# A pre-norm attention and feed-forward block on one core: seven half products for two row blocks, and q,k,v in 512 and 448 columns

## The chip, the cores and the metric

The kernel runs on one core of one Trainium2 chip. The metric is the device time of one execution in microseconds (us). The profile of one execution gives the times of its instructions; the engines are PE (matrix products), DVE and ACT (vector and scalar work), POOL, and SP, which here only issues DMAs.

## The reference

For `x` of 2048 rows and 640 columns: h = x + attention(layernorm(x)), result = h + ffn(layernorm(h)).

```python
def _A_ref(x, wqkv, wo):            # H = 32 heads of Dh = 20; W, dil = 8, 2
    qkv = (x @ wqkv) ...            # q, k, v of each head
    idx = pos[:, None] - (arange(W) * dil)[None, :]     # a row attends to itself and 7 rows before it, every second
    logits = einsum("bhsd,bhswd->bhsw", q, kg) * scale  # idx < 0 is masked
    o = einsum("bhsw,bhswd->bhsd", softmax(logits), vg)
    return o.reshape(B, S, D) @ wo

def _B_ref(x, w_gate, w_up, w_down):                    # 640 -> 1728 -> 640
    return (silu(x @ w_gate) * (x @ w_up)) @ w_down
```

Every matrix product is done in three passes: each operand is held as a rounded high part and the remaining low part, and high x high, high x low and low x high are added up in one bank. A contraction over 640 takes five chunks of 128, so a product tile takes 15 matmuls.

## The kernel before

The rows are four blocks (0 to 3) of 512; a block is four row tiles `j` of 128. `first` and `last` run q,k,v for all blocks (`qkv(b, g)`, L575): `g` is one of four column groups, each with 160 columns of q, 160 of k and 160 of v, 480 in all, four row tiles, 15 matmuls each. ACT scales and stores the product to `stage` (L580); k, v and q go to DRAM (`ksc`, `vsc`, `qsc`). Attention runs on DVE in 16 groups (block and column group): `att_qk` multiplies and reduces (L623, L628, two of each), `att_exp` and ACT's exponential (L641), `att_av` multiplies and adds (L654, L663) and turns the result (L670), which goes to DRAM as `osc` (40 KB pieces).

`wo(b)` reads `osc` back, splits it (L736 ACT, L737 DVE) and multiplies by the output weights (L747: 8 products of 15 matmuls, 320 columns); the sum with `x` is `h`; layernorm follows. Blocks 2 and 3 are turned into columns by `turn`: a 32x32 transpose on DVE (L491), four DMAs to DRAM (`xsc`, L493) and one back. `turned_columns` splits the columns into `shb` (L486, L487); blocks 0 and 1 are transposed on PE (L444, L447, L448).

`ffn(b)` goes over 14 tiles of 128 of the 1728 inner columns (the last has 64). For each, `load_ffn` reads the weights (960 KB), ACT makes the high parts (L785, L786), DVE the low ones (L802; in block 0 they are stored to `lsc`, and blocks 1 and 2 read them from there), `proj` makes gate and up (L810, 2 x 15 matmuls of 512 columns, banks 5 and 6), ACT takes silu (L844), DVE multiplies (L845), ACT and DVE split the result (L846, L848), and `down` adds 15 matmuls of 512 columns into banks 0 to 4 (L826). `finish(b)` adds `h` (L875, L879) and writes out.

All operations are recorded by `P.add(engine, cost, function, reads, writes, prio)` and ordered by `P.order()`: a list schedule with the given costs, passes backward and forward, and small seeded moves (`MOVES`). Each engine works its own list in that order, and the reads and writes become semaphore waits. So `wo(b + 1)` and the attention of later blocks lie between the tiles of block `b`. `fa`, `ra`, `sha`, `shb`, `kv` and `pq` are large areas that stages share; `kv` and `pq` belong to attention.

## Time and profile before

| | |
|---|---|
| median of 3 runs | 859.25 us (859.12 to 859.33) |
| the profiled execution | 859.15 us, its span 857.1 us |
| mean granted TensorE clock | 0.999 |
| PE busy | 850.7 us, 4007 matmuls recorded |
| DVE busy | 643.5 us |
| ACT busy | 405.7 us |
| HBM | read 140.92 MB, written 43.65 MB |

A row of a group reads: line, engine, operation, output <- input, shape, count | busy us, mean ns of one | idle us before, and who ended it. A row of the waits reads: engine, line <- who was waited for: us in total, times, longest. A row of a stretch reads: start:end, length, and busy us (count) of PE, weight loads, DVE, ACT, POOL, then granted clock, DMA share and GB/s. A row of DMA issues ends with KB of each and the median us to landing.

### The profile page before, as it was taken

The page shows a single profiled execution, that of the slowest core. Times are in us where ns is not written, and L with a number is a line of the kernel's source. Part 1 is how long each engine was busy: PE and PEld are TensorE (multiplying, and loading weights), DVE is VectorE, ACT ScalarE, POOL GpSimd, SP SyncE. Part 2 cuts the span into 40 slices and gives each one's busy share as a digit, 9 for nine tenths or more (in the row PEclk, how much of TensorE's full clock was granted, in tenths as well). Part 3 has the DMA queues.
Part 4 walks back from the last instruction along what each step waited for, and adds up shares of the span by engine and source line. Part 5 has one row for each costly group of instructions (what it writes and reads, how often), then busy time and mean ns, then how long its engine had stood idle before and what let it go on. Part 6 is the DMA issues. An engine that isn't in the chain of part 4 may idle for free.

```text
span 857.1 us, 10563 instructions
## 1 busy us (share of the span) xinstructions
PE 850.7 (99%) x4007; PEld 723.4 (84%) x4007; DVE 643.5 (75%) x705; ACT 405.7 (47%) x658; POOL 2.5 (0%) x10
## 2 busy tenths in 40 slices
PE   9999999999999999999999999999999999999998
PEld 7888888889988888988888898888888888888886
DVE  6599999999988999989999987899722326334333
ACT  6875484233762434574434548443434725233321
POOL 0000000000000000000000000000000000000000
PEclk9999999999999999999999999999999999999999
DMA  7997688569697787667999995799882756322201
GB/s 248 277 311 232 183 245 223 138 192 269 182 301 252 219 282 239 185 211 273 324 278 303 266 297 155 257 286 282 250 300 75 211 196 207 129 92 93 93 31 61
DMA packets 80018, 185.27 MB, mean 216 GB/s; under 512 B 28880, under 2 KB 42448, under 8 KB 79200
## 3 DMA queue, kind: packets, MB, share of 16 engines
q1 hardware_dynamic: 79968, 184.60, 69.9%
q8 instruction: 31, 0.51, 0.3%
q14 instruction: 19, 0.16, 0.1%
HBM read 140.92 MB, written 43.65 MB: 215 GB/s over the span
## 4 chain that ended last, share of the span: by engine, by line
PE 98%; DMA 1%; SPq 0%; ACT 0%; DVE 0%; issue 0%
PE bank L810 43%; PE bank L575 24%; PE bank L826 22%; PE bank L747 8%; PE bank L444 1%; DMA fa<-in_wqkv_dram 1%; PE bank L868 0%; PE bank L530 0%; SPq L476 0%; DVE h L875 0%; ACT ra L549 0%; ACT shb L447 0%; SPq L546 0%
## 5 line engine op out<-in xcount | busy, mean ns | idle before, releaser
L810 PE MATMUL bank<-shb,ra 128*128 128x512 f32 x1620 | 386.7, 390 | 0.4 <-ACT shb L447 0.4
L810 PEld LDWEIGHTS bank<-shb,ra 128*128 128x128 f32 x1620 | 303.4, 188 | 62.9 <-ACT shb L447 0.8
L826 PE MATMUL bank<-ra,acts 128*128 128x512 f32 x656 | 167.1, 391 | 0.0
L826 PEld LDWEIGHTS bank<-ra,acts 128*128 128x128 f32 x656 | 122.5, 188 | 24.7
L845 DVE TENSOR_TENSOR fa<-bank,fa 128x512 f32<-128x512 f32 x52 | 35.8, 689 | 107.4 <-PE bank L810 92.0
L575 PE MATMUL bank<-ra,sha 128*128 128x480 f32 x480 | 107.0, 381 | 0.2 <-ACT ra L549 0.2
L575 PE MATMUL bank<-ra,shb 128*128 128x480 f32 x470 | 103.0, 379 | 0.0
L575 PEld LDWEIGHTS bank<-ra,sha 128*128 128x128 f32 x480 | 89.4, 188 | 13.7 <-ACT ra L549 0.5
L575 PEld LDWEIGHTS bank<-ra,shb 128*128 128x128 f32 x470 | 88.1, 188 | 13.1
L785 ACT CAST ra<-fa 128x1280 fp32r<-128x1280 f32 (+1 forms) x56 | 68.5, 1224 | 50.8 <-PE bank L810 39.4
L663 DVE TENSOR_TENSOR pq<-pq 128x1280 f32<-128x1280 f32 (+2 forms) x96 | 89.7, 934 | 2.4
L623 DVE TENSOR_TENSOR pq<-kv,pq 128x2560 f32<-128x2560 f32 x32 | 90.3, 2822 | 0.9 <-DMA kv<-ksc 0.4
L654 DVE TENSOR_TENSOR pq<-kv,pq 128x2560 f32<-128x2560 f32 x32 | 90.3, 2822 | 0.7
L628 DVE TENSOR_REDUCE pq<-pq 128x128 f32<-128x2560 f32 x32 | 90.0, 2813 | 0.4
L802 DVE TENSOR_TENSOR ra<-fa,ra 128x640 fp32r<-128x640 f32 (+1 forms) x82 | 65.6, 819 | 23.2 <-ACT ra L786 21.6
L844 ACT ACTIVATE fa<-bank 128x512 f32<-128x512 f32 x52 | 31.1, 598 | 94.1 <-PE bank L810 89.3
L747 PE MATMUL bank<-ra 128*128 128x320 f32 x480 | 75.0, 310 | 0.0
L747 PEld LDWEIGHTS bank<-ra 128*128 128x128 f32 x480 | 72.0, 188 | 2.9 <-ACT fa L750 1.3
L580 ACT ACTIVATE st<-bank,fa 128x480 f32<-128x480 f32 x64 | 41.5, 662 | 67.1 <-PE bank L575 63.7
L786 ACT CAST ra<-fa 128x640 fp32r<-128x640 f32 x56 | 40.5, 726 | 59.0 <-PE bank L826 58.9
L846 ACT CAST acts<-fa 128x512 fp32r<-128x512 f32 x52 | 32.3, 621 | 58.6 <-DVE fa L845 58.5
L826 PE MATMUL bank<-acts,ra 128*128 128x512 f32 x164 | 46.1, 390 | 0.0
(88 smaller groups left out, 493.0 us busy)
## 6 DMA issues: line engine op xcount, KB each, us to landing
fa<-in_ffn_dram SPq DMA_DIRECT2D x52, 960.0 KB, 6.4
ra<-lsc SPq DMA_DIRECT2D x26, 640.0 KB, 5.3
kv<-ksc SPq DMA_DIRECT2D x32, 440.0 KB, 6.4
kv<-vsc SPq DMA_DIRECT2D x32, 440.0 KB, 7.1
ra<-lsc SPq DMA_DIRECT2D x30, 320.0 KB, 4.4
lsc<-ra SPq DMA_DIRECT2D x13, 640.0 KB, 6.0
ksc<-st SPq DMA_DIRECT2D x32, 160.0 KB, 3.2
qsc<-st SPq DMA_DIRECT2D x16, 320.0 KB, 4.0
```

What stands on the lines that cost most here:

```text
L575: T.matmul(banks[bk][:, 0:480], l, r_(wq(g, w, c), 480), start=(p, c) == first_mm, stop=(p, c) == last_mm)
L580: P.add("ACT", act(480) + 0.06, lambda bk=bk, j=j: A.activation(stage_t()[:, so : so + 1920].rearrange("p (t j c) -> p t j c", t=3, j=NJ)[ ...
L623: P.add("DVE", dve(2560), lambda: V.tensor_tensor(pq(PROD, 2560).rearrange("p (j w c) -> p j w c", j=2, w=W), window(ko, 2 * jp), pq(qo + ...
L628: P.add("DVE", dve(2560), lambda: V.tensor_reduce(pq(lo + 128 * jp, 128), pq(PROD, 2560).rearrange("p (n d) -> p n d", d=DH), axis=AX.X, o ...
L654: V.tensor_tensor(pq(PROD, 2560).rearrange("p (j n d) -> p j n d", j=2, d=DH), bass.AP(tensor=v.tensor, offset=v.offset, ap=[list(v.ap[0]) ...
L663: V.tensor_add(dst(v), v[:, :, 0:m, :], v[:, :, m : 2 * m, :])
L747: T.matmul(banks[bk][:, 0:320], l, r_(m, 320), start=p == 0 and c == 0, stop=p == 2 and c == NC - 1)
L785: P.add("ACT", act(n), lambda: A.copy(r_(gu, n), f(raw, n)), r=[rf(raw, n)], w=[rr(gu, n)], prio=PR["fh"])
L786: P.add("ACT", act(640), lambda: A.copy(r_(dn[0], 640), f(raw + n, 640)), r=[rf(raw + n, 640)], w=[rr(dn[0], 640)], prio=PR["fh"])
L802: P.add(eng, c, lambda o=o: E.tensor_sub(ra[p0:, lo + o : lo + o + 640], fa[p0:, raw + o : raw + o + 640], ra[p0:, hi + o : hi + o + 640]. ...
L810: T.matmul(banks[bk], r_(gu + 1280 * w + wid * c + col, 128), x2(a, c), start=p == 0 and c == 0, stop=p == 2 and c == NC - 1)
L826: T.matmul(banks[k], l, m, start=first and p == 0, stop=last and p == len(passes) - 1)
```

## The change

q,k,v: groups 2 and 3 together, and in blocks 1 to 3 also groups 0 and 1, are multiplied as 512 and 448 columns instead of twice 480; 32 columns of the second group's q ride with the first. They are evicted and written by an instruction of their own.

Feed-forward of blocks 2 and 3: tiles 0 to 7 of block 2 run as before (`classic`). Tiles 8 to 12 are made for both blocks at once by `pair_tile`. It splits four of the five chunks of the contraction into two halves and makes gate and up of both blocks from seven products of two chunks, with sums and differences of the weights (`N2`, `S1`, `S3`, `S4`) and of the columns of both blocks (`sums`: `T1` to `T4`, `D5`); the fifth chunk is multiplied singly (four products of one chunk). DVE adds the pieces up. Block 2's half is used at once, block 3's result goes to `psc` in DRAM and comes back in `kept_tile`, which does the down product only. Block 3 then runs tiles 13, 0 to 7 and the five kept ones.

For that, block 3 is projected earlier: `wo3` multiplies chunks 0 to 2 of the contraction (the results of column groups 0 to 2) apart from chunks 3 and 4; its layernorm takes the inverse root by steps on DVE, the rows are turned by DVE row tile by row tile, and 16 DMAs, issued in turn by SP and ACT, move them from `XN` straight to `kv`.

The order: `listed`, `forward`, `backward`, `MOVES` and what they use go, and `ORDER` holds a list for each engine. A number n is the n-th operation that the program adds for that engine, (n, m) stands for m of them from n. On PE 478 to 485 are the first part of `wo3` and 486 to 493 the second; 494 begins block 2 (six `proj` operations of tile 0; from then on 11 for each tile, six `proj` and five down operations of the tile before); 582 begins the first pair tile. On ACT 439 to 446 are the moves, from 447 on four operations belong to each of block 2's tiles (two casts, silu, split), and 489 begins the first pair tile. On DVE 325 to 360 are the rest of attention, its last two groups, 524 to 549 `wo3`, 550 to 565 multiply and split of block 2's tiles 0 to 7, 566 to 585 `sums`, and 586 begins the first pair tile.

```diff
+EARLY = 8
+QUEUES = (0, 1) * 8
...
-MOVES = [
...
+ORDER = {
+    "PE": (
...
+        498, 497, (499, 3), (503, 2), 502, (505, 2), 510, 514, 478, 509, 479, 507, 480, 511, 521, 512, 508, 519, 481, 513, (515, 2), 520, 482, (522, 3), 483,
+        518, 517, 484, 529, 528, 532, 485, 530, (525, 3), 531, 533, 486, 534, 487, 536, 488, 537, 489, 535, 490, 542, 491, 538, 541, 492, 544, 493, 543, 547,
...
+        573, 582, 581, 578, 577, (579, 2), (585, 2), (583, 2), (587, 2), 593, (589, 3), 594, 592, 602, 604, 601, (596, 3), 600, 599, 603, 595, 609, (605, 4),
...
+    "ACT": (
...
+        (430, 2), 462, (467, 2), 436, (432, 2), 471, 465, 437, 434, 466, 435, 472, 438, 469, 475, 470, 442, 445, 443, 441, 444, 446, 489, (439, 2), (490, 2),
...
+    "DVE": (
...
+        (311, 5), 483, (316, 4), 505, 484, 320, 506, 321, 485, 507, (322, 4), 508, 326, 509, (327, 4), 510, (331, 3), (511, 3), (334, 3), 517, (514, 2), 518,
+        516, (337, 4), 520, 550, 341, 523, 522, 521, (342, 2), 551, 519, 552, (524, 2), 344, 528, 553, (345, 7), 529, (352, 5), 554, 357, 555, 358, 526,
+        (359, 2), 567, 527, 568, 532, 556, 531, 557, 569, 533, 570, 534, 566, 535, 530, 540, 536, (541, 2), 537, 543, 558, (544, 3), 548, 539, 549, 559, 547,
+        560, 538, 561, (587, 3), 586, (562, 2), 575, 571, (577, 2), 572, 582, 579, 581, 564, 576, 565, 580, 574, 573, 590, (602, 2), 583, 591, 593, 604, 592,
...
+    def order(self):
+        mine, queue = {}, {}
+        for n, o in enumerate(self.ops):
+            mine.setdefault(o[0], []).append(n)
+        for e, runs in ORDER.items():
+            queue[e] = [mine[e][i] for r in runs for i in (range(r[0], r[0] + r[1]) if isinstance(r, tuple) else (r,))]
+            assert sorted(queue[e]) == mine[e]
...
         def wq(g, half, k):
-            return 4800 * g + 2400 * half + 480 * k
+            if g < 2:
+                return 4800 * half + 960 * k + 480 * g
+            return 9600 + 5120 * (g % 2) + (448 if g == 3 else 512) * (5 * half + k)
 
...
+            if b == 0 and g < 2:
+                n, shift, so = 480, 0, 1920 * g
+            else:
+                n, shift, so = ((512, 0, 0), (448, 32 if g == 1 else 0, 2048))[g % 2]
             passes = ((0, 0), (1, 0), (0, 1))
...
-                        T.matmul(banks[bk][:, 0:480], l, r_(wq(g, w, c), 480), start=(p, c) == first_mm, stop=(p, c) == last_mm)
+                        T.matmul(banks[bk][:, 0:n], l, r_(wq(g, w, c) + shift, n), start=(p, c) == first_mm, stop=(p, c) == last_mm)
...
+                if n == 448:
+                    evict(128, 448, so, 160)
+                    evict(0, 128, so + 1280, 128)
+                else:
+                    evict(0, 480, so, 160)
+                if n == 512:
+                    evict(480, 512, so + 1920, 32)
...
+            if n == 512:
+                P.add("SP", 0.65, lambda: Q.dma_start(qsc[b, g + 1, :, :, 0:32], stage_t()[:, so + 1920 : so + 2048].rearrange("p (j c) -> p j c", j=NJ)),
+                      r=[("ab", so + 1920, so + 2048)], w=[(f"Q{b}{g + 1}", 0, 1)], prio=PR["kvs"] + 1, nbytes=nb(512, 128))
...
+        def sums():
...
+            P.add("DVE", dve(1024), lambda: V.tensor_sub(pq(X2, 1024), tn(0, 2), pq(X2, 1024)), r=tnr(0, 2) + [rpq(X2, 1024)], w=[rpq(X2, 1024)], prio=0.8)
+            P.add("DVE", dve(1024), lambda: V.tensor_add(pq(T2, 1024), tn(2, 2), pq(X2, 1024)), r=tnr(2, 2) + [rpq(X2, 1024)], w=[rpq(T2, 1024)], prio=0.8)
+            put("T2", T2, 1024, 0.81)
+            put("T1", X2, 1024, 0.82)
+            P.add("DVE", dve(1024), lambda: V.tensor_add(pq(T3, 1024), tn(0, 2), tn(2, 2)), r=tnr(0, 4), w=[rpq(T3, 1024)], prio=0.83)
+            put("T3", T3, 1024, 0.83)
+            P.add("DVE", dve(512), lambda: V.tensor_sub(pq(X2 + 2048, 512), pq(X2 + 2048, 512), tn(4)), r=tnr(4) + [rpq(X2 + 2048, 512)], w=[rpq(X2 + 2048, 512)], prio=0.85)
+            column(4, 0.84)
+            P.add("DVE", dve(1024), lambda: V.tensor_sub(pq(X2 + 1024, 1024), pq(X2 + 1024, 1024), pq(T2, 1024)), r=[rpq(X2 + 1024, 1024), rpq(T2, 1024)], w=[rpq(X2 + 1024, 1024)], prio=0.86)
+            put("T4", X2 + 1024, 1024, 0.86)
+            put("D5", X2 + 2048, 512, 0.87)
+            for k, prio in ((2, 0.88), (3, 0.88), (0, 0.89), (1, 0.89)):
+                column(k, prio)
+
+        def pair_tile(i, n, between):
+            wt, W0 = PW[n % 2]
+            dn, ao = DP[n % 3], 1024 * (n % 3)
+            raw, _ = load_raw(i)
...
+            def mult(bk, o, xs, first, stop):
+                xv_, xr = xs
+                n = len(xv_)
+
+                def mm():
+                    for p, (w, a) in enumerate(PASSES):
+                        for k in range(n):
+                            T.matmul(banks[bk], ws(wt, o + 2048 * w + 128 * k, 128), xv_[k](a), start=first and p == 0 and k == 0, stop=stop and p == 2 and k == n - 1, skip_group_check=True)
+                P.add("PE", 0.687 * n, mm, r=[rws(wt, o, 128 * n), rws(wt, o + 2048, 128 * n)] + xr, w=[pb(bk)], prio=10)
...
+            a, b_, c = 5, 6, 7
+            mult(a, W0, raw_x(2, 0), True, True)
+            P.add("ACT", act(512), lambda: A.copy(Y1(), banks[a]), r=[pb(a)], w=[y1], prio=0)
+            mult(b_, N2, sum_x("T2", 2), True, True)
+            P.add("DVE", dve(512), lambda: V.tensor_add(Y2(), banks[b_], Y1()), r=[pb(b_), y1], w=[y2], prio=0)
+            mult(c, S1, sum_x("T1", 2), True, True)
+            mult(a, W0 + 256, raw_x(2, 2), False, False)
+            mult(a, W0 + 512, one(2), False, True)
+            P.add("ACT", act(512), lambda: A.activation(f(SG, 512), banks[a], AF.Silu), r=[pb(a)], w=[rf(SG, 512)], prio=0, table="silu")
+            mult(b_, S3, sum_x("T3", 2), False, False)
+            mult(b_, W0 + 896, one(3), False, True)
+            P.add("DVE", dve(512), lambda: V.tensor_add(Y3(), banks[b_], Y1()), r=[pb(b_), y1], w=[y3], prio=0)
+            P.add("DVE", dve(512), lambda: V.tensor_add(Y3(), banks[c], Y3()), r=[pb(c), y3], w=[y3], prio=0)
+            between()
+            mult(b_, W0 + 640, sum_x("T4", 2), False, False)
+            mult(b_, W0 + 896, sum_x("D5", 1), False, True)
+            P.add("DVE", dve(512), lambda: V.tensor_add(Y1(), banks[b_], Y1()), r=[pb(b_), y1], w=[y1], prio=0)
+            mult(c, S4, raw_x(3, 2), False, False)
+            mult(c, W0 + 512, one(3), False, True)
+            P.add("DVE", dve(512), lambda: V.tensor_add(Y2(), banks[c], Y2()), r=[pb(c), y2], w=[y2], prio=0)
+            P.add("DVE", dve(512), lambda: V.tensor_mul(Y1(), Y1(), f(SG, 512)), r=[y1, rf(SG, 512)], w=[y1], prio=0)
+            act_split(Y1, y1, ao, 2)
+            P.add("ACT", act(512), lambda: A.activation(Y2(), Y2(), AF.Silu), r=[y2], w=[y2], prio=0.1, table="silu")
+            P.add("DVE", dve(512), lambda: V.tensor_mul(Y3(), Y3(), Y2()), r=[y3, y2], w=[y3], prio=0.1)
+            P.add("SP", 0.45, lambda: Q.dma_start(psc[i], Y3()), r=[y3], w=[(f"P{i}", 0, 512)], prio=3, nbytes=nb(128, 2048))
+            return i, ao, dn
...
+        def kept_tile(i):
+            m = fn[0]
+            fn[0] += 1
+            dn, ao = DP[m % 3], 1024 * (m % 3)
+            so = XN + 512 * (m % 5)
+            raw, n = load_raw(i, 1)
+            P.add("SP", 0.45, lambda: Q.dma_start(f(so, 512), psc[i]), r=[(f"P{i}", 0, 512)], w=[rf(so, 512)], prio=PR["fld"], nbytes=nb(128, 2048))
+            down_hi(raw, n, dn)
+            act_split(lambda: f(so, 512), rf(so, 512), ao, 3)
+            down_lo(i, raw, n, dn)
+            return i, ao, dn
...
+        def wo3(prio):
...
+            for jp in range(2):
+                s0 = slot(3 * jp)
+                load_o(jp, 0, 2, s0, s0 + 512, 2)
+                load_o(jp, 2, 1, s0 + 1024, s0 + 1280, 3)
+                for j in (2 * jp, 2 * jp + 1):
+                    for half in range(2):
+                        product(j, half, (0, 1, 2))
+                        xo = XN + 640 * j + 320 * half
+                        P.add("ACT", act(320), lambda xo=xo: A.copy(f(xo, 320), banks[7][:, 0:320]), r=[pb(7)], w=[rf(xo, 320)], prio=PR["wev"])
+                    P.add("DVE", dve(640), lambda j=j: V.tensor_add(hs(j), hs(j), f(XN + 640 * j, 640)), r=[rf(XN + 640 * j, 640), hr(j)], w=[hr(j)], prio=prio)
...
+            for jp in range(2):
+                s0 = slot(2 * jp)
+                load_o(jp, 3, 2, s0, s0 + 512, 4)
+                for j in (2 * jp, 2 * jp + 1):
+                    for half in range(2):
+                        product(j, half, (3, 4))
+                        P.add("DVE", dve(320), lambda j=j, o=320 * half: V.tensor_add(hs(j, o, 320), banks[7][:, 0:320], hs(j, o, 320)), r=[pb(7), hr(j, 320 * half, 320)], w=[hr(j, 320 * half, 320)], prio=0.5)
+                    if j < 3:
+                        st.one(j)
+                    else:
+                        def bn():
...
+                rstd(2 * jp)
+                for j in (2 * jp, 2 * jp + 1):
+                    apply(j)
...
+            for n in range(16):
+                q, fq = n // 4, n % 4
+                eng = (Q, A)[QUEUES[n]]
+
+                def mv(q=q, fq=fq, eng=eng):
+                    eng.dma_start(kv[32 * fq : 32 * fq + 32, 2560:5120].bitcast(F32).rearrange("p (k q t) -> p k q t", k=NC, q=4)[:, :, q, :],
+                                  fa[32 * q : 32 * q + 32, XN : XN + 2560].rearrange("p (k f t) -> p k f t", k=NC, f=4)[:, :, fq, :])
+                P.add(("SP", "ACT")[QUEUES[n]], 0.5, mv, r=[rf(XN, 2560)], w=[(f"xk{fq}", 512 * k + 128 * q, 512 * k + 128 * q + 128) for k in range(NC)], prio=0.4, nbytes=nb(160, 512))
...
+        def pair(early):
+            wo3(PR["wo"])
+            d = Downs(NF)
+            for i in range(early):
+                d.put(classic(2, i, first=i == 0))
+                if len(d.pend) > 1:
+                    d.do()
+            d.do()
+            sums()
+            P.add("POOL", 0.1, lambda: G.memset(wsl_t()[:, PQ_N - 2 : PQ_N].bitcast(F32), 0.0), w=[("pq", 0, PQ_N)], prio=0)
+            n0 = fn[0]
...
+            for i in range(early, NF - 1):
+                d.put(pair_tile(i, fn[0], lambda: d.pend and d.do()))
+            d.put(classic(2, NF - 1, new=True))
+            d.do(len(d.pend))
+            finish(2)
+            d = Downs(NF)
+            for i in [NF - 1, *range(early)]:
+                d.put(classic(3, i, new=True))
+                if len(d.pend) > 2:
+                    d.do()
+            for i in range(early, NF - 1):
+                d.put(kept_tile(i))
+                if len(d.pend) > (2 if i == NF - 2 else 1):
+                    d.do()
+            d.do(len(d.pend))
+            finish(3)
...
-        last = [(2, 0), (3, 0), (2, 1), (3, 1), (2, 2), (2, 3), (3, 2), (3, 3)]
+        last = [(2, 0), (2, 1), (3, 0), (3, 1), (2, 2), (2, 3), (3, 2), (3, 3)]
```

517 lines of the change are left out of this document (278 added, 239 removed), and 77 rows, old and new, of tables (MOVES, ORDER).

## The prediction

> **What bounds the kernel now.** I read the page first, then who PE waits for, then the chain in order of time, then the groups by shape, and last DVE's stretches. The page (busy time by engine, DVE in 40 slices, the chain's shares):
>
> ```profile
> span 857.1 us, 10563 instructions
> ...
> PE 850.7 (99%) x4007; PEld 723.4 (84%) x4007; DVE 643.5 (75%) x705; ACT 405.7 (47%) x658; POOL 2.5 (0%) x10
> ...
> DVE  6599999999988999989999987899722326334333
> ...
> PE 98%; DMA 1%; SPq 0%; ACT 0%; DVE 0%; issue 0%
> PE bank L810 43%; PE bank L575 24%; PE bank L826 22%; PE bank L747 8%; PE bank L444 1%; DMA fa<-in_wqkv_dram 1%; PE bank L868 0%; PE bank L530 0%; SPq L476 0%; DVE h L875 0%; ACT ra L549 0%; ACT shb L447 0%; SPq L546 0%
> ```
>
> PE is the chain: gate and up products (L810), q,k,v (L575), down (L826), output projection (L747). All that PE waits for:
>
> ```profile
> PE bank L459 <- POOL ra L892: 1.4, 1, 1.4
> PE bank L530 <- DVE fa L406: 0.5, 1, 0.5
> PE bank L810 <- ACT shb L447: 0.4, 1, 0.4
> PE bank L575 <- ACT ra L549: 0.2, 1, 0.2
> ```
>
> That is 2.5 us, none of it after the first tile. So a matmul taken away is time gained, and a wait put in is time lost. The chain in order of time (start, length, what, how many) gives the price of a matmul:
>
> ```profile
> 54.18 58.34 PE bank L575 x270
> 189.26 8.79 PE bank L747 x60
> ...
> 556.99 1.13 PE bank L810 x5
> ...
> 630.47 2.19 PE bank L747 x15
> ...
> 714.48 13.63 PE bank L810 x60
> ```
>
> 480 columns cost 58.34/270 = 0.2161 us, 320 columns 8.79/60 = 0.1465, 512 columns 13.63/60 = 0.2272. At 556.99 block 2 (the third) begins its feed-forward.
>
> **Seven half products.** A classic tile has 2 x 15 matmuls of 512 columns for each block, 60 for two. `pair_tile` calls `mult` with two chunks seven times (6 matmuls each) and with one chunk four times (3 each): 42 + 12 = 54. Six fewer in five tiles: 30 x 0.2272 = 6.8 us off the path. The down products stay.
>
> **512 and 448 columns.** The number of matmuls stays; in seven pairs of column groups (one in block 0, two in each other block), 4 row tiles x 15 = 60 pairs each, 420 pairs of 480 + 480 become 512 + 448. No row has 448. The straight line through 320 and 512 rises 0.0807/192 = 0.00042 us a column; it gives 0.2138 at 480, where the trace has 0.2161, and 0.2003 at 448. So 480 is 2.3 ns dearer than its neighbours. If 448 lies on the line, a pair costs 0.4275 instead of 0.4322: 420 x 0.0047 = 2.0 us. If 448 bears the same 2.3 ns, 1.0 us; on the line from 480 through 512 (0.205), nothing. I take 2.0: 320 and 448 are multiples of 64 as 512 is, 480 isn't. ACT gets a second eviction in 56 places. It is busy 30.5 of 50 us in the fullest stretch of that stage (fourth pair of figures), and a product's bank comes round only after five products, so I cost it at nothing; with that room gone it would be some 0.3 us a place.
>
> ```profile
> 100.00:150.00 50.00, 50.00 (x242) 43.57 (x242) 48.81 (x48) 30.52 (x58) 0.00 (x0) 1.00 0.82 220
> ```
>
> The Trainium skill (TensorE: Matmul & The Clock Gate, Back-to-back issue gap) speaks against this part: it has a warm matmul's gap as N/2.4 + 2.5 ns, which is linear, so that 512 + 448 costs what 480 + 480 does. By it this part would give 0. The trace disagrees in the size (0.2161 us at 480 against its 0.2025) and in the straightness.
>
> **The sum.** 6.8 + 2.0 = 8.8. The profiled execution took 859.15 us (span 857.1 and 2.05 around it), 0.1 below the median of the runs, 859.25. Without new waits: 850.35.
>
> **Where new waits may come: the fourth block is needed earlier.** Before, the fourth block's output projection runs at 630.47 and later, spread over the third block's tiles, and its columns are wanted only at 714. Now `wo3` multiplies three chunks between tiles 1 and 3 of the third block, and the last two chunks around tile 4 (operations 486 to 493 of the written PE order stand between 533 and 543). PE gets there thus: block 2 starts at 556.99 + 0.9 (the last bits of block 1) - 2.0 = 556; tiles 0 to 3, three downs and one product of tile 4 are 120 + 45 + 5 matmuls x 0.2272 = 38.6; nine matmuls x 8 of `wo3` x 0.1465 = 10.5: 605. The half that needs the very last attention result comes 8 us later, 613. It needs the result written out, read and split:
>
> ```profile
> osc<-pq SPq DMA_DIRECT2D x128, 40.0 KB, 4.3
> fa<-osc SPq DMA_DIRECT2D x16, 256.0 KB, 4.7
> ...
> xsc<-fa SPq DMA_DIRECT2D x8, 320.0 KB, 4.9
> fa<-xsc SPq DMA_DIRECT2D x2, 1280.0 KB, 8.3
> ```
>
> 4.3 + 4.7 and about 1.3 for ACT's and DVE's split (groups below): DVE must end attention by 603. Now it ends at 622, and between the first tile and there DVE looks so:
>
> ```profile
> 249.00:622.00 373.00, 373.00 (x1743) 314.18 (x1742) 338.39 (x346) 178.22 (x261) 0.73 (x2) 1.00 0.84 257
> ...
> DVE fa L845 <- PE bank L810: 12.3, 11, 2.1
> DVE pq L647 <- ACT pq L641: 4.3, 3, 2.7
> ...
> 564.84 0.69 DVE L845 TENSOR_TENSOR fa<-bank,fa 128x512 f32<-128x512 f32 x1
> ...
> 569.36 2.82 DVE L623 TENSOR_TENSOR pq<-kv,pq 128x2560 f32<-128x2560 f32 x1 [0.42 <-DMA kv<-ksc]
> ...
> 603.46 0.69 DVE L845 TENSOR_TENSOR fa<-bank,fa 128x512 f32<-128x512 f32 x1 [2.19 <-ACT fa L844]
> ...
> 615.79 2.82 DVE L654 TENSOR_TENSOR pq<-kv,pq 128x2560 f32<-128x2560 f32 x1
> ...
> 621.56 0.51 DVE L670 STREAM_TRANSPOSE pq<-pq 128x320 f32<-128x320 f32 x1
> ```
>
> DVE is busy 338.4 of 373 us (the third pair of figures), idle 34.6. The work up to attention's end hardly changes (three tiles' multiplies and subtractions fewer, six at 0.69; `wo3`'s first adds and splits more, about as much). With no idle time it ends at 249 - 2 + 338 = 585, with the old idle time at 620, 17 us late, and the PE order can't go round it. What decides is the order. Of the 34.6 us the largest item, 12.3, is the multiply L845 queued in front of attention work and waiting for PE (2.19 at 603.46), and 4.3 is a wait for the exponential; a wait for DMA is rare (0.42 at 569.36). Such waits a written order can avoid. At the multiply of block 2's tile 0 (564.84) eight of the 96 long attention instructions (L623, L628, L654) are still to come now, from 569.36 to 615.79; in the new DVE list four come behind the same operation, and the last attention operation stands right behind tile 2. Four times 2.82, with the adds between, is over 14 us further on at the same place of PE. I take it that DVE arrives about when PE does.
>
> **Second narrow place: rows turned on chip and sums.** The round trip through DRAM (4.9 + 8.3 above) goes, and 16 moves of 80 KB go from `XN` to `kv`, eight from SP and eight from ACT. SP's four similar ones before (three, then one) occupy its queue:
>
> ```profile
> 678.88 2.17 SPq L493 DMA_DIRECT2D xsc<-fa  x3
> ...
> L802 DVE TENSOR_TENSOR ra<-fa,ra 128x640 fp32r<-128x640 f32 x80 | 63.9, 819 | 19.8 <-ACT ra L786 18.2 <-ACT ra L785 1.5
> L663 DVE TENSOR_TENSOR pq<-pq 128x1280 f32<-128x1280 f32 x32 | 47.7, 1490 | 0.8
> L848 DVE TENSOR_TENSOR acts<-fa,acts 128x512 fp32r<-128x512 f32 x52 | 35.7, 687 | 7.9 <-ACT acts L846 7.8
> L640 DVE TENSOR_TENSOR pq<-pq 128x256 f32<-128x256 f32 x16 | 6.8, 425 | 0.5
> L736 ACT CAST ra<-fa 128x512 fp32r<-128x512 f32 x16 | 9.8, 618 | 2.9 <-PE bank L747 2.0 <-DMA fa<-osc 0.8
> L844 ACT ACTIVATE fa<-bank 128x512 f32<-128x512 f32 x52 | 31.1, 598 | 94.1 <-PE bank L810 89.3 <-PE bank L868 4.5
> ```
>
> About 0.72 us each, so 5.8 us of ACT's queue. In ACT's list they stand between the cast of tile 5 and the silu of tile 6, with three casts of the first pair's weights; the first of these must wait until tile 6's products have read the weights it overwrites. Counting PE on from 613: tile 6's products end at 638, ACT's silu of tile 6 comes behind a cast (0.7), two moves (1.4), and casts of 1.0, 0.5 and 0.7 (scaled from L736's 0.62 at 512 columns), and takes 0.6 itself: done at 643, where tile 7's first product wants that bank at 641. That is 0 to 2 us of PE. The last moves land at about 638 + 2 + 4.5 = 644.5; then DVE's list has the sums up to the low half of T2: six operations of 1024 columns at 1.2 (between the rows of 640 and 1280), five of 512, two multiplies of tile 7's kind, 13.5 us, and a weight split of 1.2: 659. PE wants it for the second half product at 638 + 21 = 659. So again 0 to 2 us, if the moves land as fast as the rows say. I put 1.2 us for both together: 851.6.
>
> From there DVE has room. A pair tile costs it 0.82 x 2 + 0.69 + 0.43 x 2 + 1.2 + 0.55 for weights and 8 x 0.69 for the combination, 10.5 us, where PE needs (54 + 15) x 0.227 = 15.7. The five kept tiles of the last block have downs alone, 15 x 0.227 = 3.4 us each; each needs a 320 KB weight load and 256 KB of kept activations, and DVE 1.5 us. Their buffers are two deep for weights, which with 4.9 us to land (320 KB, above) just holds. DVE's busy time in these stages before (second pair, 10.9 and 17.4 of 50) says that the room is there:
>
> ```profile
> 650.00:700.00 50.00, 50.00 (x239) 42.45 (x238) 10.90 (x17) 24.82 (x41) 0.00 (x0) 1.00 0.55 177
> 750.00:800.00 50.00, 50.00 (x222) 41.44 (x221) 17.42 (x24) 14.47 (x19) 0.00 (x0) 1.00 0.28 99
> ```
>
> The first load, the start and the end keep their form; I give them 0.
>
> **The rivals.** (1) The forecast: 30 matmuls and the cheaper columns, small waits, 849.3 to 852.5: 0.52.
> (2) 448 lies on the line through 480 and 512, at 0.205, and gives back what 512 adds: 2.0 us less gain, 853.6 with the same waits. For it: no row of 448. Against: 480 lies off the line of 320 and 512. 0.13. The linear rule of the Trainium skill's page named above is this case.
> (3) The pair's sums or moves come late: if the moves take 8.3 us to land like the old read back and ACT's queue costs its 2, then 850.35 + 4 + 2, 854 to 857.5. For it: both places above have no slack. 0.16.
> (4) Attention comes late and PE waits for it around tiles 2 to 4 of the third block: slower. Priced by the old idle time: 17 us, 867; each us of DVE idle time over 18 in that stretch costs one. It decides from 10.5 us of lateness, that is 28 us of the 34.6 kept. For it: DVE was the fullest engine there, and a written order can't go round a late operation. Against: most of those waits are by order, not by data. 0.14. Between, 7.2 to 10.5 us late: no change, 0.05.
>
> **How the numbers follow.** 0.2% (1.7 us, about what a measurement of this kernel can tell) puts no change between 857.5 and 861. Faster: 0.52 + 0.13 + 0.16 = 0.81; same 0.05; slower 0.14. The range from 849.3 (the sum without waits, less 1 us for a 448 still cheaper than the line) to 859.0 leaves out most of (4) alone. The likeliest is 851.6.
>
> **What would show it.** Right: 1590 matmuls in the gate, up and half products instead of 1620; spacing of 0.200 at 448 columns; PE's waits on others below 2 us between 550 and 670; attention's last transpose near 600. Wrong: a wait of PE for DVE or ACT in the projection of block 3 (rival 4), at the second half product of the first pair tile or the start of tile 7 (rival 3), or 448 columns at 0.203 and more (rival 2).

## The result: slower by 0.9%, and where the time is

The changed kernel takes 867.45 us (median of 4 runs, 864.78 to 867.76) against 859.18 us for the kernel before (859.04 to 859.33): ratio 1.0089, 95% interval 1.0069 to 1.0109. The forecast was 851.6. The page of the profiled execution (busy time, DVE in 40 slices, the chain's shares):

```profile
span 865.7 us, 10685 instructions
...
PE 854.5 (99%) x3977; PEld 718.9 (83%) x3977; DVE 697.4 (81%) x807; ACT 412.1 (48%) x722; POOL 3.3 (0%) x12
...
DVE  5599999999999899998999899999667865553333
...
PE 97%; ACT 1%; DVE 1%; DMA 1%; issue 0%; SPq 0%; ACTq 0%; DVEq 0%
```

PE is still the chain. It has 30 matmuls fewer (3977 for 4007) and yet is busy 3.8 us longer (854.5 against 850.7): matmuls have become longer. All that PE waits for:

```profile
PE bank L481 <- DVE sha L484: 1.8, 1, 1.8
PE bank L407 <- POOL ra L1185: 1.4, 1, 1.4
PE bank L812 <- ACT shb L395: 1.2, 1, 1.2
PE bank L481 <- DVE fa L354: 0.8, 1, 0.8
PE bank L392 <- DVE shb L396: 0.7, 1, 0.7
PE bank L536 <- ACT ra L529: 0.6, 1, 0.6
PE bank L812 <- ACT fa L847: 0.4, 1, 0.4
PE bank L536 <- ACT sha L483: 0.3, 1, 0.3
```

7.2 us against 2.5 before, and none at a place that the forecast feared: no row names the early projection (L1054), the half products (L977) or the moves. Now the price of a matmul, in PE's groups by shape (the last figure before the bar on the right is the mean ns of one; matmuls overlap, so it is longer than their spacing, but it moves with it), first before, then after:

```profile
L810 PE MATMUL bank<-shb,ra 128*128 128x512 f32 x1620 | 386.7, 390 | 0.4 <-ACT shb L447 0.4
L826 PE MATMUL bank<-ra,acts 128*128 128x512 f32 x656 | 167.1, 391 | 0.0
```

```profile
L812 PE MATMUL bank<-shb,ra 128*128 128x512 f32 x1050 | 254.5, 393 | 1.6 <-ACT shb L395 1.2 <-ACT fa L847 0.4
L827 PE MATMUL bank<-ra,acts 128*128 128x512 f32 x656 | 173.8, 396 | 0.0
L536 PE MATMUL bank<-ra,shb 128*128 128x512 f32 x240 | 55.8, 390 | 0.0
...
L536 PE MATMUL bank<-ra,sha 128*128 128x512 f32 x180 | 43.2, 397 | 0.0
...
L812 PE MATMUL bank<-kv,wsl 128*128 128x512 f32 x120 | 29.7, 395 | 0.0
```

The same product of 512 columns takes 390 to 393 when it reads `ra` and `shb` alone (the 393 has seven matmuls at half clock in it), and 395 to 397 when `acts`, `sha` or `wsl` takes part. Measured from start to start, intervals over 260 ns left out: 227.4 ns for `ra,shb`, 228.4 for `shb,ra`, but 232.8 for `ra,acts`, 231.3 for `acts,ra`, 232.3 for `ra,sha`, 232.7 for `kv,wsl`. Before, none is over 227.2.

Adding up every interval between two starts, less what a matmul of its width normally takes, gives the account. From first to last matmul, 851.5 us became 860.1, 8.6 more: 7.7 less for 30 matmuls and the new widths; 9.0 more for intervals a few ns too long; 7.2 more for gaps and matmuls at half clock (13.9 against 6.7), of which 1.8 in the first 50 us, 4.0 from 200 to 300 us, 1.4 from 550 to 600 us.

### The profile page after: what moved, and what is told of

The parts are those of the page before. It is cut to its first block, busy times and chain, and to the rows that moved or that the text cites. A ratio compares the mean times of both kernels' runs of the same rounds, so it can differ in the third digit from the quotient of the medians.

```text
span 865.7 us, 10685 instructions
## 1 busy us (share of the span) xinstructions
PE 854.5 (99%) x3977; PEld 718.9 (83%) x3977; DVE 697.4 (81%) x807; ACT 412.1 (48%) x722; POOL 3.3 (0%) x12
## 4 chain that ended last, share of the span: by engine, by line
PE 97%; ACT 1%; DVE 1%; DMA 1%; issue 0%; SPq 0%; ACTq 0%; DVEq 0%
PE bank L812 35%; PE bank L536 24%; PE bank L827 21%; PE bank L977 7%; PE bank L724 6%; PE bank L1054 2%; PE bank L392 1%; DMA fa<-in_x_dram 1%; PE bank L481 0%; PE bank L1161 0%; ACT L847 0%; ACT L618 0%; ACT ra L793 0%; ACT shb L395 0%; DVE fa L352 0%
## 5 line engine op out<-in xcount | busy, mean ns | idle before, releaser
L812 PE MATMUL bank<-shb,ra 128*128 128x512 f32 x1050 | 254.5, 393 | 1.6 <-ACT shb L395 1.2
L812 PEld LDWEIGHTS bank<-shb,ra 128*128 128x128 f32 x1050 | 197.5, 189 | 44.8 <-ACT shb L395 1.4
L536 PE MATMUL bank<-ra,sha 128*128 128x512 f32 (+2 forms) x480 | 107.9, 382 | 0.3 <-ACT sha L483 0.3
L536 PE MATMUL bank<-ra,shb 128*128 128x512 f32 (+1 forms) x470 | 102.7, 378 | 0.0
L788 DVE TENSOR_TENSOR ra<-fa,ra 128x640 fp32r<-128x640 f32 x70 | 56.3, 819 | 27.8 <-ACT ra L778 25.0
L543 ACT ACTIVATE st<-bank,fa 128x480 f32<-128x480 f32 (+3 forms) x120 | 50.6, 474 | 57.1 <-PE bank L536 42.3
L793 ACT CAST ra<-fa 128x1280 fp32r<-128x1280 f32 (+1 forms) x41 | 50.1, 1221 | 24.1 <-PE bank L812 18.0
L724 PE MATMUL bank<-ra 128*128 128x320 f32 x360 | 56.4, 309 | 0.0
L724 PEld LDWEIGHTS bank<-ra 128*128 128x128 f32 x360 | 54.3, 188 | 1.9 <-ACT fa L727 0.5
L848 DVE TENSOR_TENSOR fa<-bank,fa 128x512 f32<-128x512 f32 x42 | 28.8, 686 | 30.7 <-PE bank L812 21.3
```

Of the source, the lines that this page charges most:

```text
L536: T.matmul(banks[bk][:, 0:n], l, r_(wq(g, w, c) + shift, n), start=(p, c) == first_mm, stop=(p, c) == last_mm)
L543: P.add("ACT", act(m) + 0.06, lambda: A.activation(stage_t()[:, o : o + NJ * m].rearrange("p (t j c) -> p t j c", j=NJ, c=w)[:, :, j, :], ...
L724: T.matmul(banks[bk][:, 0:320], l, r_(m, 320), start=p == 0 and c == 0, stop=p == 2 and c == NC - 1)
L788: P.add("DVE", tt(640), lambda o=o: V.tensor_sub(ws(t, lo + o, 640)[p0:], fa[p0:, raw + o : raw + o + 640], ws(t, hi + o, 640)[p0:].bitcas ...
L793: P.add("ACT", act(n), lambda: A.copy(ws(wt, gu, n), f(raw, n)), r=[rf(raw, n)], w=[rws(wt, gu, n)], prio=PR["fh"])
L812: T.matmul(banks[bk], ws(wt, gu + 1280 * w + wid * c + col, 128), x(a, c), start=p == 0 and c == 0, stop=p == 2 and c == NC - 1)
```

## The experiments

Each was run beside the kernel before on the same chip.

**e1_pad: `pq`, `sha` and `acts` back on multiples of 256 bytes.** The change allocates `kv` (5280 columns of 4 bytes, 82.5 times 256 bytes) ahead of `pq`, `sha` and `acts` instead of last. By the built programs those areas start at a multiple of 256 bytes before, and 128 bytes past one after.

```diff
-        kv = sb.tile([128, KV_N], F32R, name="kv")
+        kv = sb.tile([128, KV_N + 32], F32R, name="kv")
```

> The changed kernel with the area kv made 32 columns (128 bytes) longer, so that pq, sha and the activations behind it begin at a multiple of 256 bytes again; nothing else. Place theory (an operand area that begins at an odd multiple of 128 bytes costs each matmul that reads it 5.7 ns): spacing of the down products back from 232.5 to 227 ns, total 9.1 us less, about 858.3 us. Rival, order theory (the matmuls are slower because the written order mixes them otherwise with the other engines' traffic): spacing stays at 232, about 867 us. In both the waits of PE near 8, 240 to 251 and 555 us stay, some 7 us.

859.03 us (before 859.12; ratio 1.0, interval 0.9991 to 1.0009). The groups are back:

```profile
L827 PE MATMUL bank<-ra,acts 128*128 128x512 f32 x656 | 170.3, 390 | 0.0
...
L812 PE MATMUL bank<-kv,wsl 128*128 128x512 f32 x120 | 29.0, 389 | 0.0
```

32 unused columns give 8.4 us of the median back (in the account, 8.5 of the 9.0); the order stayed, so the rival that blamed the order is out. What remains against before is the gain of 7.7 and gaps of 14.2 instead of 6.7.

**e2_before_128 and e3_before_64: the same slip in the kernel before.** `shb` 32 or 16 columns longer, so that all areas behind it slip by 128 or 64 bytes; nothing else.

```diff
-        shb = sb.tile([128, 5120], F32R, name="shb")
+        shb = sb.tile([128, 5152], F32R, name="shb")
```

> The kernel before with the area shb made 32 columns (128 bytes) longer, so that pq, sha and the activations begin at an odd multiple of 128 bytes as in the changed kernel; its order stays. Place theory: 820 down matmuls x 5.7 ns = 4.7 us and the 480 q,k,v matmuls that read sha 1 to 2.6 us, so 865 to 866.5 us. Order theory: 859.2 us.

> The kernel before with shb 16 columns (64 bytes) longer. Place theory, if the limit is 256 bytes: any odd start costs the same, about 865 to 866.5 us; if it is the distance in 128 byte halves that counts, between 859.2 and that. Order theory: 859.2 us.

864.80 us (ratio 1.0065, 1.005 to 1.008) and 867.47 (1.0095, 1.0078 to 1.0112). The first lies just under its forecast, the second over both of its own, and for 64 bytes only the time is known, not which products pay. In e2:

```profile
L575 PE MATMUL bank<-ra,sha 128*128 128x480 f32 x480 | 106.9, 380 | 0.0
...
L826 PE MATMUL bank<-ra,acts 128*128 128x512 f32 x656 | 170.6, 395 | 0.0
```

The down products pay (232.6 ns from start to start); the products of 480 columns with `sha`, which has slipped as well, don't (216.1; before 216.3). Half of them read weights that start 128 bytes past a multiple even in the kernel before, and are no slower (215.7 against 216.3 for the other half). Nor do 448 columns with `sha` in the changed kernel (203.9 there and in e1). So the loss is not the change's arithmetic: the place alone makes it, in the old kernel too. Only products of 512 columns are seen to pay; why the narrower ones don't is open. The surcharge of 480 columns is not one of place.

**e8_acts_128: one area alone.** As e1, with `sha` 32 columns longer, so that only `acts` lies at 128 bytes.

```diff
-                late["sha"] = sb.tile([128, 5120], F32R, name="sha", tag="sha")
+                late["sha"] = sb.tile([128, 5152], F32R, name="sha", tag="sha")
```

> The changed kernel with kv 32 columns longer and the area behind it (sha) 32 columns longer: only the activations of the feed-forward start at 128 bytes past a multiple of 256, all other areas on a multiple. Place theory: each operand is charged by itself. The down products that have acts as the stationary operand (about 650) are 5.7 ns longer, those that stream it (about 160) 4.2, together 4.4 us: 863.4; gate, up, q,k,v at 227.2. Rival, that what counts is how many areas are off or which bytes two operands share: no change (859.0) or the full 9 us (868).

866.65 us (4 runs, 863.91 to 868.06; ratio 1.0083, 1.0063 to 1.0103); the profiled execution is the 863.91.

```profile
L827 PE MATMUL bank<-ra,acts 128*128 128x512 f32 x656 | 173.9, 396 | 0.0
...
L536 PE MATMUL bank<-ra,sha 128*128 128x512 f32 x180 | 42.3, 392 | 0.0
...
L812 PE MATMUL bank<-kv,wsl 128*128 128x512 f32 x120 | 29.1, 390 | 0.0
```

What touches `acts` is dear, and `sha` and `wsl` no longer are: each operand is charged by itself. Against e1 it is 5.5 ns from start to start where `acts` is the stationary operand, 4.6 where it is streamed. The gate or up matmul just ahead of a down product with `acts` stationary is longer too (232.5 against 226.9, 52 of them), so part of the charge falls ahead of the matmul itself. The other gate and up matmuls are 0.9 ns longer though none of their operands moved; in e2 they are as well (227.9 against 227.0, some 1.5 of its 5.7 us). That stays open. The profiled run lies 0.5 us over the forecast of 863.4, but the median 3.3: the two runs at 868 had a mean granted clock of 0.994, the profiled one 0.998. By an estimate from these figures 0.4% of 866 us is 3.5 us, so most of that difference is clock and not place.

**e4_order: three edits of the written order by eye.** On e1: the order of the start as before, the first tile's preparation earlier, one silu earlier.

```diff
-        ... 171, 172, 173, 376, 174, 378, 377, 175, 397, 396, 176, 395, 379, 402, 380, 382, ...   (DVE)
+        ... 171, 172, 376, 173, 378, 379, 377, 380, 174, 175, 397, 396, 176, 395, 402, 382, ...
```

> The padded kernel with three edits of the written order alone: the first 70 PE operations and the operations of DVE, ACT and SP that belong to them in the order of the kernel before; the third addition, the inverse root and the casts for the columns of block 0 ahead of attention and weight casts; block 1's silu of tile 12 ahead of an exponential. Theory (those three waits are the rest of the loss): 858.3 less 2 at the start, 3 at 240 to 251 and 1 at 555, about 852. Rival (the waits move to the next late operation): over 856.

868.68 us (ratio 1.0115, 1.0097 to 1.0132): 9.7 us worse than e1. What PE waits for now:

```profile
PE bank L538 <- DVE ra L510: 4.1, 1, 4.1
PE bank L814 <- DVE shb L398: 3.2, 1, 3.2
PE bank L829 <- DVE acts L862: 1.4, 1, 1.4
```

The forecast of 852 missed; each wait came back larger at the next operation. The first is not one of the lists' order at all. `order()` writes the program out engine by engine in turns; a read or write of a bank then meets, in the program, accesses that happen much later, to other parts of the same bank, and gets waits for them. Here DVE stood 5.0 us behind a cast that it doesn't need.

**e5_emit: written out by time.** On e1, every engine's list unchanged:

```diff
-                    out.append(q[at[e]])
+                    start[n] = max([free[e]] + [end[d] for d in deps])   # end and free from the costs
...
-        return out
+        return sorted(out, key=start.get)
```

> The changed kernel with kv 32 columns longer (all areas on multiples of 256 bytes), the order on every engine as the change has it, and one thing more: the instructions of the five engines are written out in the order of their estimated start times instead of engine by engine in turns. The order on each engine is the same; what differs is which write of a bank the program sees before which read, and with that a few waits. In the changed kernel the transposes of the second row tile into bank 5 wait for a subtraction that reads another part of bank 5 (1.8 us at the start); written out in time order they wait only for the statistics. Writing-out theory: 1 to 1.5 us less than the same kernel without this (859.0), so 857.5 to 858. Rival, data theory: the transposes wait for the late load of x anyway, and the next product for its weights: no change, 859.0.

858.34 us (ratio 0.9988, 0.9979 to 0.9997). PE at the start, after and in e5:

```profile
10.12 0.76 PE L481 MATMUL bank<-fa 128*128 128x128 f32 x5 [1.85 <-DVE sha L484]
```

```profile
8.32 0.71 PE L486 MATMUL bank<-fa 128*128 128x128 f32 x5
```

The transposes of the second row tile write another part of bank 5 than the subtraction reads; their wait for it goes. The first 50 us lose 4.6 instead of 6.2 (before: 4.2). It is a wait that no data asks for. The medians, 859.03 and 858.34, differ by less than either kernel's runs spread (857.76 to 860.96 in e1), so the gain rests on the trace.

**e6_first, e7_both, e9_mult, e10_silu, e11_load, e12_pe: chasing the waits at the first tile.** All on e5; of each edit the lines that matter are shown. e6 moves the last transposes on PE and the steps of DVE and ACT that belong to them, e7 takes the start's order as well; e9 adds DVE's multiply, e10 two silus, e11 the weights' loads and more of DVE, e12 (on e10) PE's second and third tile.

```diff
-  PE   148, 149, 150, 135, 139, 151, 152, 161        +  148, 149, 150, 135, 151, 152, 139, 161       (e6)
-  DVE  177, 178, 179, 180, 181, 398                  +  177, 398, 178, 179, 180, 181                 (e9)
-  ACT  204, 192, 187, 188, 274, 281, 280, 278        +  192, 187, 188, 274, 204, 278, 281, 280       (e10)
-  SP   349, 198, 199, 348, 353, 115, 116, 113, 112, 356   +  353, 349, 198, 199, 348, 356, 115, 116, 113, 112   (e11)
-  PE   178, 171, 172                                 +  171, 172, 178                                (e12)
```

> As e5_emit, with one stretch of the written order changed, around the first feed-forward tile (235 to 250 us): the residual sum of the last row tile goes ahead of the attention product, its statistics ahead of the column casts; the two last groups of transposes go ahead of the last q,k,v product on TensorE instead of behind it; the second tile's weight casts go behind the columns. In this kernel's trace without the edit TensorE waits there 0.75 + 0.86 + 1.45 = 3.1 us. Order theory: these go, and nothing takes their place, as the transposes and casts now lie beside 3.4 us of products: 2 to 3 us less than e5_emit, 855 to 856. Rival, that the waits move: DVE's subtractions of the last columns, which must wait for the last q,k,v product, now come last, 1 us or more: under 1 us gained.

> As e6_first, with the first 70 TensorE operations and what goes with them on the other engines in the order that the kernel before has (x is loaded ahead of the weights). Before loses 4.2 us in the first 50 us against back-to-back matmuls, the changed one 6.0 to 6.2. Order theory: 0.5 to 2 us less than e6_first, 854 to 855; the first attempt at this order failed at the writing out (a subtraction waited 5.0 us for a cast that it does not need), which is repaired here. Rival: the weights arrive later in this kernel as its loads are cut differently, and TensorE waits for them at 8 to 12 us: as e6_first or 1 to 3 us more.

> As e6_first, with two more steps of the written order moved: DVE's multiply of the first tile goes ahead of an attention sum of 2.8 us (in e6_first TensorE waits 2.5 us for it and then runs 8 matmuls at 427 ns), and in the second block's last tile but one the silu goes ahead of attention's exponential and its two table loads (0.67 and 0.28 us there). Order theory: e6_first had moved the wait from the columns to this multiply; with it gone the 2.6 + 1.5 + 0.9 us go, 853.5 to 855, and the kernel beats before by 0.5%. Rival, that DVE has no room: attention, put back by each of these steps, comes late in the third block or the wait moves once more: 857 or more.

> As e6_first with the first tile's multiply ahead of the attention sum (as in e9_mult) and without e9_mult's edit in the second block (there TensorE waited 1.4 us at 555 for the last tile's split). New: ScalarE's silu of the first tile goes ahead of attention's exponential, and the silu of the second tile ahead of two casts that wait for the third tile's weights, which land 7 us after their issue. In e9_mult TensorE waited 0.6 and 1.9 us for these two silus. Order theory: both waits go and the next operation, the casts of the third tile, has room for it: 4 us less than e6_first and e9_mult, 854 to 855. Rival, that there is always a next late operation (the third tile's weights, landing at 253, two casts and three splits of them, are wanted at 255 to 257): 1 to 2 us of the 2.5 come back: 856.5 to 858.

> As e10_silu, where TensorE now waited 2.3 us for a cast of the third tile's weights (loaded at 245.6 behind four stores in SP's list, landed at 252.5) and 1.0 us for the second tile's multiply. The loads of the third and fourth tile go ahead of the stores and the evictions' stores in SP's list, and the second tile's multiply and the third tile's splits of gate and up go ahead of the rest of that attention group on DVE. Order theory: the load is issued when its buffer is free, at 243.6, two us earlier, and both waits go: 3 to 4 us less than e10_silu, 854 to 855. Rival, one late operation after the other: the wait turns up at the fourth tile (its weights, or attention's rows on DVE), 857 to 858, and what this stretch costs is the work packed into it, not one step's place.

> As e10_silu (not e11_load), where TensorE waited 2.3 us at 252 for the third tile's gate weights and 1.0 us at 260 for the second tile's multiply. Now TensorE's own order is changed: the last two operations of the second tile (10 matmuls, 2.3 us) go ahead of the third tile's first product; that tile's gate cast goes ahead of its down cast, its load ahead of four stores, and DVE's multiply of the second tile ahead of three weight splits, behind the attention group that e11_load had pushed it through. Order theory: the weights land at 252.0, are cast by 254.0 and wanted at 254.1, and both waits go: 3 us less than e10_silu, 854 to 855.5, the first version that beats both kernels by 0.4%. Rival, DVE is full here (62 of 65 us from 235 to 300 in e10_silu), and any step put ahead makes another late: a wait of 1 us or more for DVE between 256 and 290, 857 to 859.

858.62, 859.49, 858.45, 857.96, 862.96 and 860.41 us; ratios 0.9994 (0.9985 to 1.0003), 1.0001 (0.9992 to 1.0011), 0.9995 (0.9984 to 1.0007), 0.999 (0.9981 to 0.9999), 1.0042 (1.0028 to 1.0056), 1.0009 (1.0 to 1.0018). All six missed their forecasts of 853.5 to 856; their rivals, that the wait moves on, fit, and e11 and e12 came out above even the rivals' times. In e7, e4's order of the start written out by time, e4's wait of 4.1 us for DVE is gone (the longest for DVE there is 1.1), as the writing out would have it; but the start gains nothing. Of each other one, the longest wait of PE, in the order e6, e9, e10, e11, e12:

```profile
PE bank L820 <- DVE fa L856: 2.5, 1, 2.5
```

```profile
PE bank L820 <- ACT fa L855: 2.5, 2, 1.9
```

```profile
PE bank L820 <- ACT ra L801: 2.3, 1, 2.3
```

```profile
PE bank L835 <- DVE acts L850: 4.5, 1, 4.5
```

```profile
PE bank L835 <- ACT acts L849: 3.9, 1, 3.9
```

Columns, multiply, silu, the third tile's weights, then the split of activations: nearly every edit took away the wait that it was made for (in e11, 1.3 of the weights' 2.3 us stayed), and the longest one stood one operation further on. Five misses of the same kind suggest that something behind them all has a fixed time. The first split of activations has one, within 2 us. Last stores from the staging area (first and last start, us), before and after:

```profile
L595 SPq DMA_DIRECT2D qsc<-st x2: 587/590/592, 236.5 to 246.3; - x2
```

```profile
L556 SPq DMA_DIRECT2D vsc<-st x4: 445/458/588, 247.4 to 258.8; - x4
```

and ScalarE's splits of activations between 235 and 275 us, before and after:

```profile
L846 ACT CAST acts<-fa x3: 622/622/622, 249.9 to 267.3; 128x512 fp32r<-128x512 f32 x3
```

```profile
L841 ACT CAST acts<-fa x3: 610/622/623, 264.3 to 269.9; 128x512 fp32r<-128x512 f32 x3
```

The same from the other traces:

| | before | after | e1 | e5 | e6 | e9 | e10 | e12 |
|---|---|---|---|---|---|---|---|---|
| last store of q,k,v issued, us | 246.3 | 258.8 | 257.6 | 256.2 | 259.3 | 258.9 | 258.5 | 258.7 |
| first split on ACT | 249.9 | 264.3 | 263.2 | 263.0 | 264.2 | 264.5 | 263.6 | 264.9 |
| first gate product | 241.3 | 246.8 | 245.7 | 244.1 | 241.6 | 241.2 | 240.7 | 240.7 |
| first down product | 255.7 | 268.9 | 266.3 | 264.7 | 267.3 | 265.4 | 265.0 | 265.6 |

`acts` and the staging area of q,k,v share memory (both have the tag `ab`), and a split must wait until the last store from there has landed. The trace bears this out: by the built program POOL's memset of two columns of `acts` waits for the same landings as the split and for nothing else that is late, and in each of these traces the two start within 0.4 us of each other. In the changed kernel, beside the split at 264.3:

```profile
L1221 POOL MEMSET acts<- x1: 100/100/100, 264.4 to 264.4; 128x2 f32 x1
```

90 gate and up matmuls (20.4 us) lie between the first gate and the first down product (60 before), so a gate product that starts before 244 only lengthens the wait: in these versions no down product runs before 264.7. In the changed kernel itself and in e1 PE doesn't wait for the split (in e5 0.2 us); there it loses its time around the first gate product, to waits for a copy and for the columns (0.6 + 0.7 + 1.2 us). The shared area is why taking those away brought nothing.

**e13_stores: the area earlier.** On e12: three evictions go ahead on ACT, the six stores of the 512-column results ahead on SP.

```diff
-  ACT  247, 272, 273, 191, 197, 196, 277, 276, 192, 187, 188, 274
+       247, 272, 187, 188, 273, 192, 191, 197, 196, 277, 276, 274
-  SP   353, 349, 198, 199, 348, 115, 116, 113, 112, 356, 110, 108, 114, 107, 351, 106, 111, 109
+       198, 199, 110, 108, 107, 353, 106, 111, 109, 349, 348, 115, 116, 356, 113, 112, 114, 351
```

> As e12_pe, with the last results of q,k,v evicted and stored earlier: the evictions of the last 512-column product go on ScalarE from behind the second tile's weight casts to right behind the first tile's gate cast, and their six stores go in SP's list ahead of the stores and loads that wait for the first tile's splits. In all versions of the changed kernel so far the first split of activations starts at 262.2 to 264.9 us (before: 249.9), whatever TensorE's waits ahead of it, because the activations lie in the area from which q,k,v results are stored, and the last of these stores is issued at 256 to 260 (before: 246.3). Theory, the shared area sets the first down product: stores issued by 252 to 254, the first split at 258 to 260, the first down product at 261.3 without the 4.1 us wait of e12_pe and the half clock behind it: 6 us less than e12_pe, 853.5 to 855. Rival, DVE or the weights set it: the wait at the first down product keeps 3 us or more, now for DVE or a load: 857 or more.

859.30 us (ratio 1.0, 0.9991 to 1.0009). What touches `acts` between 235 and 275 us (min/median/max ns, first and last start) in e12 and in e13:

```profile
L849 ACT CAST acts<-fa x3: 610/617/622, 264.9 to 268.8; 128x512 fp32r<-128x512 f32 x3
L850 DVE TENSOR_TENSOR acts<-fa,acts x3: 685/692/693, 265.6 to 272.9; 128x512 fp32r<-128x512 f32 x3
```

```profile
L849 ACT CAST acts<-fa x3: 610/618/619, 261.0 to 268.5; 128x512 fp32r<-128x512 f32 x3
L850 DVE TENSOR_TENSOR acts<-fa,acts x3: 650/684/692, 265.3 to 272.7; 128x512 fp32r<-128x512 f32 x3
```

The last store is issued at 252.8, and ACT's split comes 3.9 us earlier, as the shared area would have it. DVE's half doesn't follow (265.3): in its list it stands behind four attention steps and a weight split. PE's wait of 3.9 us stays, now for L850, and the forecast of 853.5 to 855 missed; the rival, that DVE sets it, named this wait.

**e14_split: and the list with it.**

```diff
-  ACT  281, 284, 275        +  281, 275, 284
-  DVE  182, 183, 411, 184, 185, 186, 399        +  182, 399, 183, 411, 184, 185, 186
```

> As e13_stores, where the last store of q,k,v was issued at 252.8 instead of 258.7, but the first split of activations still came at 261.0 on ScalarE (behind a weight cast that waited until 259.2 for a load) and at 265.3 on DVE (behind four attention steps and a weight split), so that TensorE waited 3.9 us at its first down product and ran 7 matmuls at 427 ns behind it. Now both halves of that split go ahead: on ScalarE ahead of the cast, on DVE right behind the attention product that ends at 260.5. Theory, the area set it and then the order written for it: with both changed the first down product runs at 261.5 to 262.5 without a wait, 5 us less than e13_stores, 853.5 to 855.5. Rival, the stores land only at 261 (as the 0.5 us wait for a DMA suggests): 1 us of wait remains, 855.5 to 857. Third, DVE's attention, now later by one step, makes the next down products late: 857 or more.

856.51 us (11 runs, 855.55 to 859.38): ratio 0.9975, 0.9966 to 0.9984, the lowest of all versions (e5 and e10 lie 0.1% below the kernel before). The forecast of 853.5 to 855.5 missed.

```profile
PE bank L835 <- DVE acts L850: 1.3, 1, 1.3
```

```profile
262.19 1.04 PE L835 MATMUL bank<-acts,ra 128*128 128x512 f32 x3
```

The first down product runs at 262.2 without a wait; 1.3 us comes back at the second tile's split. The time lies in the first rival's range, and the stores do land only at 261, as it has it: the split still starts when the area is free, beside POOL's memset,

```profile
L849 ACT CAST acts<-fa x3: 611/621/623, 261.1 to 268.3; 128x512 fp32r<-128x512 f32 x3
L1229 POOL MEMSET acts<- x1: 101/101/101, 261.2 to 261.2; 128x2 f32 x1
```

but the wait that remains is one for DVE. Gaps are 10.5 us in all, 3.7 less than in e1, still 3.8 over before: of the 7.7 us gained, 2.6 are kept by the medians.

## Why the prediction was wrong, point by point

- **Seven half products, 6.8 us: right.** 3977 matmuls are recorded against 4007, and without the slip (e1) each of 512 columns takes 226.7 to 227.5 ns.
- **512 and 448 columns, 2.0 us: mis-sized by half.** 448 columns measure 202.6 ns from start to start with `shb`, and 203.9 with `sha`, not the 200.3 of the line through 320 and 512. With `shb` a pair takes 429.8 against 432.2: 420 times 2.5 ns is 1.0 us, and that is at most. It is the bound "448 bears the same 2.3 ns", which the prediction had and didn't choose. Rival 2 is not borne out either: it needs 205, at which 512 and 448 would cost what 480 and 480 do; the half with `sha` does pass the 0.203 that was its sign.
- **The step that failed first: what the change moves.** The prediction goes through the change part by part and has no line for the allocation of `kv`, which the change moves from last to fourth, with a length that isn't a multiple of 256 bytes. So the sum prices every matmul left as if it cost what it did before (0.2272 us for 512 columns), a term put at nothing without a reason. Price: 9.0 us in the account, shown by e1 (given back), e2 and e3 (made in the old kernel), e8 (one area alone).
- **"The first load, start and end keep their form; I give them 0": failed, 1.8 us.** The edit that replaced `order()` was read as a change of lists. It also changed how the lists are woven into one program, and so the waits; e5 takes most of it away by its trace, and e4 shows how large it can be (4.1 us).
- **The first tile of block 0, 4.0 us: no line in the prediction.** In the changed kernel these are the waits for a copy and for the columns (0.6 + 0.7 + 1.2 us), the seven matmuls at half clock behind them (1.4 us) and small gaps. Which part of the change made them late was not separated.
- **"I cost it at nothing" of the second evictions, with busy time of a stretch as the reason: too short.** Their results share an area with the activations, and the last store of q,k,v went from 246.3 to 258.8. e13 and e14 show that this and the order behind it bind the first tile once the waits ahead of it are gone. A new order alone brought the last store back to 252.8; how much of the rest is the split into two evictions is open.
- **Rival 4, attention late: the lateness came, the wait didn't.** Attention's last transpose is at 609.7 ("near 600"), the second part of the projection at 618 to 633 (forecast: from 605, its last half from 613), and PE has no row of waits for it. PE was late itself: block 2 begins at 568 instead of the forecast 556. But in e14, where PE comes 7 us earlier, attention ends earlier too (last transpose at 602.4, the second part from 610.6), again without a wait. That DVE arrives about when PE does held.
- **The second narrow place, 1.2 us: nothing.** The gaps from 600 to the end add up to less than 0.5 us. One sum there is off by its own rows, without consequence: six operations at 1.2, five and two at 0.69 are 12.0 us, not 13.5.
- From 550 to 600 us, not forecast, 1.4 us, most of it at 555: ScalarE (ACT) runs attention's exponential between two silus, with a table load of 1.28 us on either side, as the chain shows:

```profile
552.15 1.28 ACT L618
553.88 1.28 ACT L847
```

  e9 put the silu first and then waited 1.4 us for the last tile's split; that edit was dropped.

The errors add up: 851.6 + 9.0 (place) + 7.2 - 1.2 (waits) + 1.0 (448) = 867.6; measured 867.45. The account was made from the trace afterwards, so that it closes proves nothing by itself; the 9.0 are shown by experiments. That the result lies near rival 4's 867 is chance.

## What to carry to other kernels

When a diff moves an allocation, work out the byte at which each area starts before and after: here a slip of 128 bytes cost more (9.0 us) than 30 matmuls brought (6.8). Read the code that weaves engine lists into a program as part of the schedule. And when a wait reappears one operation further on after each repair, stop repairing and look for what has the same time in all the traces.

## What the runs showed of the hardware

**Place.** A matmul of 512 columns takes 226.7 to 227.5 ns from start to start when all operands begin at a multiple of 256 bytes (e1), 232.3 to 233.0 with the stationary one at 128 bytes past it, 231.0 to 231.7 with the streamed one there (the changed kernel, e2, e8); 480 columns don't change (216.1 to 216.3), and the kernel with areas at 64 bytes is slower still (867.47 against 864.80 us). The Trainium skill (SBUF — State Buffer, Operand start alignment) asks only that an operand start at a multiple of its element size, and adds: "This is about legality, not speed". Every area here meets that rule; the price stands beside it.

**Half clock after short gaps.** In the changed kernel three gaps of 0.6, 0.7 and 1.2 us, within 7 us, were followed by 7 matmuls at 427 ns, 1.4 us more. The mean granted clock (the figure ahead of the last two) of that stretch is 0.89:

```profile
240.00:255.00 15.00, 12.65 (x52) 10.31 (x53) 14.75 (x22) 12.80 (x20) 0.00 (x0) 0.89 0.97 280
```

e1 has the same three gaps and no slow matmul, e10 a gap of 2.4 us and none, e6 2.6 us and 8 slow ones (384 to 427 ns), beginning 1.3 us after PE resumed. The one run of the changed kernel with a granted clock of 1.0 took 864.78 us, the three at 0.996 to 0.998 took 867.4 to 867.8: so up to 2.7 us of its median may be this chance. The Trainium skill (TensorE: Matmul & The Clock Gate, What's actually happening) has the clock halved after an idle window of about 3.4 us that runs freely. The chance and the delay agree with a free-running window; that gaps of 2.6 us and less were enough doesn't follow from it.
